# Attention and expert kernel on one core: pair 30's score inputs and pair 26's probabilities moved ahead in the hand-written lead-in table, pair 32's scaling moved behind

## Chip, cores and metric

The kernel runs on one core of a Trainium2 chip. The metric is the time of one execution on the device in microseconds (us); the kernel before has a median of 714.67 us over three runs.

## What is computed

Banded attention with a few global keys, then a feed-forward layer with a rational activation, all in float32:

```python
# q, k, v: (4, 8, 768, 64); n_global = 8, n_local = 96
rel = pos[:, None] - pos[None, :]
keep = (pos[None, :] < n_global) | ((rel >= 0) & (rel < n_local))
scores = scale * (q @ k.T) - slopes[h] * dist        # dist = |rel|, n_local for far global keys
a = softmax(where(keep, scores, -1e9)); x = a @ v
x = x.transpose(0, 2, 1, 3).reshape(3072, 512)
# the feed-forward layer: d_model 512, d_ff 2048
h = x @ w_in
P = a[0] + a[1]*h + a[2]*h*h + a[3]*h**3
Q = 1 + |b[0]|*|h| + |b[1]|*h*h
out = (P / (Q + 1e-6)) @ w_out
```

## The kernel before

The 3072 tokens are 12 chunks of 256. A chunk has eight attention units (two token tiles by four pairs of heads; units are numbered 0 to 95) and eight feed-forward steps (128 x 2 columns of `d_ff` each, numbered 0 to 95 as well). From unit 24 on two units are handled together and named by the even one: "pair 30" is units 30 and 31, four heads of one token tile. The feed-forward of a chunk runs about one chunk behind its attention, so TensorE has large matmuls to do while the softmax of later pairs is made on the other engines.

What happens to one such pair u, with the words of the table that names each stage:

- `L` loads q and k into `nat` (lines 179, 180); `V`, `vp` load v.
- `sp` (`st_split`): POOL scales q in `nat` (line 505), then DVE transposes `nat` in 32 x 32 blocks into `sp` (line 508).
- `zw` (`st_scatter`, line 516): SP sends `sp` to a DRAM buffer `zq` in four transfers. `sr` (`st_gather`, line 523): SP reads it back as `qk`, the layout that the score matmuls want. There are two `zq` buffers, used by turns.
- `s` (`st_score`, line 598): 56 small matmuls (32 for the first tile of a batch) from `qk` into PSUM. `t` (line 633): DVE adds the mask, takes the row's extreme. `x` (line 642): ACT's exponential. `r` (lines 647, 649): DVE's sum and reciprocal. `n` (line 655): POOL scales the probabilities `pr`.
- `T` (`st_pT`, line 675): DVE transposes `pr` in blocks. `tw` (`st_spread`, line 686): SP sends them to DRAM buffer `z` in four transfers. `P` (`st_pTE`, line 702): SP reads them back as `pT`.
- `o` (line 721): the matmuls of two pairs with v; `y`, `z` (lines 750, 760) make the two-part `xh`, `xl` that feeds the feed-forward steps.

One feed-forward step f: `f1` (line 340, 24 matmuls into `h`), `e1` (lines 372 to 374, ACT), `e2` (381, 382, DVE), `eq` (386, POOL, in a few steps DVE: `SUM_V`), `e3` (397, 398, ACT), `e4` (402 to 404, DVE), `gh` (412, ACT), `gl` (415, POOL or DVE), then `f2` (line 442, six matmuls for each of the two token tiles) two steps later. The result of step f that `f2` waits for is called g18, g19 and so on here, the sum of `eq` fa18, the step's PSUM result h18.

What sets the order: PE and SP execute in the order in which the program issues their work. Until step 30 of the main loop the order on ACT, DVE and POOL is written by hand too: `LEAD` is one string of words, each word a stage of a unit, read left to right under `manual_schedule`. What the table has issued, the loop skips (`part` keeps a set `done`). From then on a scheduler places the work of ACT, DVE and POOL by the priorities in `PRI`, with `behind` holding the scaling `sp` behind the last `eq` or `gl` on POOL once `paced["on"]` is set.

The end of the table is where the chunk's first pairs of the new kind (24, 26, 28, 30, 32) pass through these stages while the feed-forward steps 14 to 18 run. Lines of the change: the last three lines of `LEAD` (78 to 80), and line 859, `paced["on"]`.

Of the kernel before, what the change touches and what calls it, by code (L numbers as in the profile page):

```python
# [34 lines left out]
FIXED = 30  # L35
# [39 lines left out]
f1_1_5_1 z20 li23 e4_1_4 T23 e1_1_5 P23 s24 li13 t24 f2_0_7_0 t25 sr26 eq_1_5 e2_1_5 x24 f2_0_7_1 e3_1_5  # L75
ho11 lo9 o22 O0_0 lo11 f1_1_6_0 y22 O0_1 gh_1_4 z22 ho12 D0_1 gl_1_4 e4_1_5 f1_1_7_0 f1_1_7_1 r24 D0_0
n24 gh_1_5 f1_1_6_1 gl_1_5 e1_1_7 lo10 f2_1_4_0 e1_1_6 eq_1_7 L30 e2_1_7 e2_1_6 f2_1_4_1 L32
x25 eq_1_6 f1_2_0_0 r25 lo12 e3_1_6 f1_2_0_1 n25 e4_1_6 s26 t26 f2_1_5_0 x26 t27 T24 tw24 sr28 r26 ho13 e3_1_7 n26 lo13 f1_2_1_0 e1_2_0 e4_1_7 f2_1_5_1 eq_2_0 gh_1_6 f1_2_1_1 s28 x27 gl_1_6 e3_2_0 r27 P24
f2_1_6_0 e2_2_0 n27 kG26 t28 x28 e1_2_1 e4_2_0 f2_1_6_1 eq_2_1 e2_2_1 f2_1_7_0 f2_1_7_1 gh_2_0 gl_2_0 O1_0 O1_1
r28 n28 sp30 zw30 D1_0 T26 tw26 ho14 lo14 V28 D1_1 V30 V32 ho15 lo15  # L80
"""


# [59 lines left out]
def tile_kernel(ctx: ExitStack, tc: tile.TileContext, q, k, v, n_global, n_local,  # L143
# [202 lines left out]
    paced = {}  # L346
# [4 lines left out]
    def behind(engine):  # L351
        return tc.issue_after(paced[engine]) if paced.get("on") else nullcontext()
# [6 lines left out]
    def plain(f):  # L359
        return (f < FPC or divmod(f, FPC) in PLAIN) and not pl.split  # L360
# [62 lines left out]
    def cut_of(c):  # L423
        return HALF if c < 2 and not pl.split else FPC
# [281 lines left out]
    def run_of(u):  # L706
        return 4 if u >= PAIRS else 2
# [56 lines left out]
    def windowed():  # L764
# [26 lines left out]
        def part(kind, *args):  # L791
            if (kind, *args) not in done:
                done.add((kind, *args))
                parts[kind](*args)

        def token(word, final=False):
            kind = word[:2] if word[:2] in parts else word[0]
            rest = word[len(kind):]
            if kind == "BL":
                part(kind)  # L800
                return
            if kind in "Wabcdhl":
                part(kind, (1, int(rest[1]), int(rest[2])) if rest[0] == "i" else (0, int(rest[1:])))
                return
            args = [int(x) for x in rest.split("_") if x]
            if not final and kind in ("f1", "f2", "e1", "e2", "eq", "e3", "e4", "gh", "gl"):
                args = [FPC * args[0] + args[1], *args[2:]]
            part(kind, *args)
# [10 lines left out]
        for t in range(NU + LAG + F2):  # L819
            k = t - LAG  # L820
            u0 = t - 3 - run_of(t - 4)

            def on(name, u, *kinds):
                if 0 <= u < NU:
                    tc.cur_priority = base + 1000 * t + PRI[name]
                    for kind in kinds:
                        part(kind, u)

            def ffn(name, k, kind, *args):
                if 0 <= k < NU:  # L830
                    tc.cur_priority = base + 1000 * t + PRI[name]
                    part(kind, steps[k], *args)

            def ffn2(name, k, x):
                if 0 <= k < NU:
                    c, j = divmod(steps[k], FPC)
                    tc.cur_priority = base + 1000 * t + PRI[name]
                    part("f2", steps[k], x)
                    if j == cut_of(c) - 1 and j < FPC - 1:
                        part("H", c, x)  # L840
                    if j == FPC - 1:
                        part("O", c, x)
                        if c < NCH - 1:
                            late.append((c, x))
                        else:
                            part("D", c, x)

            def on_send(c, x):
                tc.cur_priority = base + 1000 * t + PRI["load"]
                part("D", c, x)  # L850

            if k == NU - 2:
                with tc.manual_schedule(engines={mybir.EngineType.Activation, mybir.EngineType.DVE, mybir.EngineType.Pool, mybir.EngineType.SP}):
                    for n, word in enumerate(TAIL.split()):
                        tc.cur_priority = base + 1000 * t + n
                        token(word, True)
                break
            fixed = t >= FIXED
            paced["on"] = t >= FIXED
            if t % 2:  # L860
                on("gather", t + 1, "sr")
                on("load", t + 3, "zw")
                on("load", t - 3, "P")
            else:
                on("load", t + 6, "L")
                on("load", t, "V")
                on("load", t - 2, "vp")
            if t < FIXED:
                on("score", t - 2, "s", "kg", "t")
                on("soft", t - 2, "x", "r")  # L870
            if fixed and t % 2:
                on("score", t - 1, "s", "t")
                on("score", t, "t")
                if u0 % 4 == 0:
                    on("pv", u0, "o")
                    on("x", u0, "y", "z")
            ffn("ffn1a", k, "f1", 0)
            if t < FIXED:
                on("qkT", t, "qT")
                if u0 % run_of(t - 4) == 0:  # L880
                    on("pv", u0, "o", "vg")
                    on("x", u0, "y", "z")
                on("qkE", t, "qE", "kG")
            ffn("ew3", k - 1, "e3")
            if t < FIXED:
                on("norm", t - 2, "n")
            ffn("ffn1b", k, "f1", 1)
            ffn("ew1", k, "e1")
            ffn("ew4", k - 1, "e4")
            if 0 < k <= NU and not plain(steps[k - 1]):  # L890
                ffn("ew4", k - 1, "gh")
                ffn("ew4", k - 1, "gl")
            ffn("ew2", k, "e2")
            ffn("ew2", k, "eq")
            if t % 2 == 0:
                with behind(mybir.EngineType.Pool):
                    on("split", t + 4, "sp")
                    on("split", t - 2, "kG")
            if fixed:
                on("score", t - 1, "t")  # L900
                for u in (t - 1, t) if t % 2 else (t - 1,):
                    on("soft", u, "x", "r")
                    on("norm", u, "n")
            on("pT", t - 2, "T", "tw")
            for c, x in late:
                on_send(c, x)
            late.clear()
            if t < FIXED:
                on("pT", t - 3, "P")
            ffn2("ffn2a", k - F2, 0)  # L910
            ffn2("ffn2b", k - F2, 1)
            for key in [(1, ct, jw) for jw in range(4) for ct in range(NCT)] + [(0, ft) for ft in range(NFT)] if t == FIXED else ():
                tc.cur_priority = base + 1000 * t + PRI["wsplit"]
                for kind in "Wabcdhl":
                    part(kind, key)
# [99 lines left out]
    with ExitStack() as es:  # L1015
        pl.dram = es.enter_context(tc.tile_pool(name="dram", bufs=1, space=bass.MemoryType.DRAM))
        zs[:] = [pl.dram.tile([2 * P, NB * P], F32, tag=f"z{n}", name=f"z{n}", bufs=1) for n in range(2)]
        zqs[:] = [pl.dram.tile([P, NB, P], F32, tag=f"zq{n}", name=f"zq{n}", bufs=1) for n in range(2)]
        pl.ldp = es.enter_context(tc.tile_pool(name="ldp", bufs=2))
        pl.att = es.enter_context(tc.tile_pool(name="att", bufs=2))  # L1020
        pl.ffn = es.enter_context(tc.tile_pool(name="ffn", bufs=2))
        pl.ps_h = es.enter_context(tc.tile_pool(name="ps_h", bufs=2, space=PSUM))
        pl.ps_o = es.enter_context(tc.tile_pool(name="ps_o", bufs=2, space=PSUM))
        pl.ps_r = es.enter_context(tc.tile_pool(name="ps_r", bufs=1, space=PSUM))
        pl.ps_t = es.enter_context(tc.tile_pool(name="ps_t", bufs=3, space=PSUM))
        windowed()
# [51 lines left out]
```

## Time and profile before

| what | value |
|---|---|
| median of 3 runs | 714.67 us (713.19, 714.67, 715.09) |
| the profiled execution's own time | 712.47 us |
| its span, first to last instruction | 710.7 us |
| mean granted TensorE clock | 0.985 of full speed |
| busy: PE, DVE, ACT, POOL | 671.8, 537.8, 532.3, 361.9 us |

The profile is of one execution, by a hardware profiler. Times in its views are in us from the start of the span. "Idle before" is the time in which the engine had nothing running, with the instruction that ended it; that releaser is inferred, and where several things were waited for the last one by the profile is named. SPq is the queue of transfers that SP issues: its rows are the issues, and the landing comes later.

### The profile page before, as it was taken

The page shows a single profiled execution, that of the slowest core. Times are in us where ns is not written, and L with a number is a line of the kernel's source. Part 1 is how long each engine was busy: PE and PEld are TensorE (multiplying, and loading weights), DVE is VectorE, ACT ScalarE, POOL GpSimd, SP SyncE. Part 2 cuts the span into 40 slices and gives each one's busy share as a digit, 9 for nine tenths or more (in the row PEclk, how much of TensorE's full clock was granted, in tenths as well). Part 3 has the DMA queues.
Part 4 walks back from the last instruction along what each step waited for, and adds up shares of the span by engine and source line. Part 5 has one row for each costly group of instructions (what it writes and reads, how often), then busy time and mean ns, then how long its engine had stood idle before and what let it go on. Part 6 is the DMA issues. An engine that isn't in the chain of part 4 may idle for free.

```text
span 710.7 us, 17118 instructions
## 1 busy us (share of the span) xinstructions
PE 671.8 (95%) x6167; PEld 576.8 (81%) x6167; DVE 537.8 (76%) x1319; ACT 532.3 (75%) x1174; POOL 361.9 (51%) x487
## 2 busy tenths in 40 slices
PE   5799997999939999999999999999999999999995
PEld 4577776868738898888888898888888888899995
DVE  6898996897856777777778778778687777766664
ACT  6899998686727787787777777777777777776763
POOL 2444546565434555555565455546555456444441
PEclk9999999899979999999999999999999999999998
DMA  8874554412177567475376584674566755420001
GB/s 197 260 216 109 171 157 133 128 44 62 40 198 169 141 166 174 124 201 137 88 187 142 134 219 120 148 196 107 131 162 159 175 135 149 126 88 1 30 1 36
DMA packets 161215, 95.22 MB, mean 134 GB/s; under 512 B 100064, under 2 KB 141152, under 8 KB 161120
## 3 DMA queue, kind: packets, MB, share of 16 engines
q1 hardware_dynamic: 161120, 94.02, 51.0%
q8 instruction: 51, 0.84, 0.5%
q14 instruction: 44, 0.36, 0.2%
HBM read 66.39 MB, written 27.59 MB: 132 GB/s over the span
## 4 chain that ended last, share of the span: by engine, by line
PE 79%; ACT 11%; DVE 3%; issue 2%; SPq 2%; DMA 1%; POOL 1%; POOLq 0%; ACTq 0%
PE h L340 33%; PE acc L442 30%; PE o L721 6%; PE s L598 4%; PE acc L438 2%; PE h L332 2%; ACT pr L642 2%; ACT r L271 1%; ACT fu L372 1%; DMA r<-in_moe_w_in_dram 1%; ACT qzero L561 1%; PE s L584 1%; ACT fs L397 1%; ACT fa L373 1%; ACT q L398 1%
## 5 line engine op out<-in xcount | busy, mean ns | idle before, releaser
L386 POOL TENSOR_TENSOR fa<-fa,fs 128x512 f32<-128x512 f32 (+1 forms) x86 | 109.8, 1277 | 161.2 <-ACT fs L374 156.8
L397 ACT ACTIVATE fs<-fa,coef 128x512 f32<-128x512 f32 (+1 forms) x97 | 69.9, 721 | 86.3 <-POOL fa L386 82.9
L655 POOL TENSOR_SCALAR pr<-pr,stats 128x160 f32<-128x160 f32 (+2 forms) x170 | 67.9, 417 | 127.8 <-DVE stats L649 75.9
L442 PE MATMUL acc<-wout_h,g 128*128 128x512 f32 x352 | 117.1, 393 | 0.7 <-POOL g L415 0.7
L402 DVE SCALAR_TENSOR_TENSOR fu<-fu,coef,q 128x512 f32<-128x512 f32 (+1 forms) x97 | 71.7, 739 | 60.2 <-ACT q L398 59.8
L415 POOL TENSOR_TENSOR g<-fu,g 128x512 fp32r<-128x512 f32 x84 | 107.9, 1285 | 15.4 <-ACT g L412 11.5
L442 PE MATMUL acc<-h,g 128*128 128x512 f32 x336 | 110.7, 391 | 0.0
L340 PE MATMUL h<-xh,win_h 128*128 128x256 f32 x352 | 101.8, 289 | 0.2 <-DVE fu L382 0.2
L340 PE MATMUL h<-xh,h 128*128 128x256 f32 x352 | 101.2, 287 | 0.0
L340 PE MATMUL h<-xl,win_h 128*128 128x256 f32 x352 | 98.7, 280 | 0.6 <-DVE xl L760 0.6
L340 PE MATMUL h<-xl,h 128*128 128x256 f32 x352 | 98.4, 280 | 0.0
L642 ACT ACTIVATE pr<-pr,stats 128x160 f32<-128x160 f32 (+2 forms) x192 | 82.6, 433 | 17.7 <-DVE stats L633 17.7
L372 ACT ACTIVATE fu<-h,coef 128x512 f32<-128x512 f32 x94 | 73.0, 776 | 27.7 <-PE h L340 26.5
L381 DVE TENSOR_TENSOR fu<-fu,h 128x512 f32<-128x512 f32 (+1 forms) x97 | 65.8, 678 | 35.6 <-ACT fs L374 34.5
L442 PEld LDWEIGHTS acc<-wout_h,g 128*128 128x128 f32 x352 | 66.1, 188 | 13.3 <-POOL g L415 1.2
L382 DVE SCALAR_TENSOR_TENSOR fu<-fu,coef,h 128x512 f32<-128x512 f32 (+1 forms) x97 | 71.2, 734 | 2.7
L442 PEld LDWEIGHTS acc<-h,g 128*128 128x128 f32 x336 | 63.1, 188 | 11.9 <-issue 0.2
L403 DVE SCALAR_TENSOR_TENSOR q<-fa,coef,q 128x512 f32<-128x512 f32 (+1 forms) x97 | 72.2, 744 | 0.0
L340 PEld LDWEIGHTS h<-xh,win_h 128*128 128x128 f32 x352 | 66.4, 189 | 4.6 <-issue 1.9
L340 PEld LDWEIGHTS h<-xh,h 128*128 128x128 f32 x352 | 66.2, 188 | 4.2 <-issue 2.8
L340 PEld LDWEIGHTS h<-xl,win_h 128*128 128x128 f32 x352 | 66.5, 189 | 2.1 <-DVE xl L760 0.8
L404 DVE SCALAR_TENSOR_TENSOR fu<-q,fu 128x512 f32<-128x512 f32 (+1 forms) x97 | 66.3, 683 | 2.2
(262 smaller groups left out, 1683.2 us busy)
## 6 DMA issues: line engine op xcount, KB each, us to landing
pT<-z SPq DMA_DIRECT2D x30, 512.0 KB, 4.1
z<-T SPq DMA_DIRECT2D x120, 80.0 KB, 2.3
zq<-sp SPq DMA_DIRECT2D x144, 64.0 KB, 1.8
qk<-zq SPq DMA_DIRECT2D x36, 256.0 KB, 2.8
r<-in_moe_w_in_dram SPq DMA_DIRECT2D x16, 512.0 KB, 5.3
r<-in_moe_w_out_dram SPq DMA_DIRECT2D x16, 512.0 KB, 3.9
nat<-in_q_dram SPq DMA_DIRECT2D x48, 128.0 KB, 4.3
nat<-in_k_dram SPq DMA_DIRECT2D x48, 128.0 KB, 4.2
```

The lines of the kernel that those rows point to most:

```text
L340: nc.tensor.matmul(out=h_of(f, y), lhsT=w[:, fs], rhs=x[:, ct, :], start=(n == 0), stop=(n == 3 * NCT - 1))
L372: nc.scalar.activation(out=u, in_=h, func=AF.Identity, scale=a3, bias=a2)
L382: nc.vector.scalar_tensor_tensor(out=u, in0=u, scalar=a1, in1=h, op0=ALU.add, op1=ALU.mult)
L386: pace(side(f, SUM_V).tensor_tensor(out=a, in0=a, in1=s, op=ALU.add))
L397: nc.scalar.activation(out=s, in_=a, func=AF.Ln, bias=q1)
L402: nc.vector.scalar_tensor_tensor(out=u, in0=u, scalar=a0, in1=r, op0=ALU.add, op1=ALU.mult)
L403: nc.vector.scalar_tensor_tensor(out=r, in0=a, scalar=q1, in1=r, op0=ALU.add, op1=ALU.mult)
L404: nc.vector.scalar_tensor_tensor(out=u, in0=r, scalar=2.0, in1=u, op0=ALU.subtract, op1=ALU.mult, reverse0=True)
L415: pace(side(f, G_V, f == NU - 1 and ys == 1).tensor_tensor(out=gs[f][:, 1, ys], in0=ew[f]["u"][:, ys], in1=gs[f][:, 0, ys], op=ALU.subtract))
L442: nc.tensor.matmul(out=acc, lhsT=gs[f][:, z, y, ts], rhs=w, start=(start and n == 0), stop=(stop and n == 2))
L642: nc.scalar.activation(out=d, in_=d, func=AF.Exp, scale=-1.0, bias=st[:, x:x + 1], accum_out=st[:, 2 + 2 * x:3 + 2 * x])
L655: (nc.vector if u < NORMS else nc.gpsimd).tensor_scalar(out=d, in0=d, scalar1=st[:, 6 + x:7 + x], scalar2=0.0, op0=ALU.mult, op1=ALU.add)
```

## The change

The table's words are permuted and a few are added. `sp30 zw30` (pair 30's scaling, transpose and scatter) move from the table's last line to the start of its third last, right behind the loads `L30` and `L32`. `P24` (which stood at the end of that line) and a new `sr30` (pair 30's gather) stand right behind `sr28`. `T26 tw26` move from the last line up behind `t28`, and a new `P26` with them. In the kernel before, `sr30` and `P26` were not in the table and came from the main loop. The pacing of `sp` starts two loop steps earlier; step 28's `sp32` is then held behind the last `eq` or `gl` on POOL.

```diff
-x25 eq_1_6 f1_2_0_0 r25 ... T24 tw24 sr28 r26 ho13 ... e3_2_0 r27 P24
-f2_1_6_0 e2_2_0 n27 kG26 t28 x28 e1_2_1 ... O1_0 O1_1
-r28 n28 sp30 zw30 D1_0 T26 tw26 ho14 lo14 V28 D1_1 V30 V32 ho15 lo15
+sp30 zw30 x25 eq_1_6 f1_2_0_0 r25 ... T24 tw24 sr28 P24 sr30 r26 ho13 ... e3_2_0 r27
+f2_1_6_0 e2_2_0 n27 kG26 t28 T26 tw26 P26 x28 e1_2_1 ... O1_0 O1_1
+r28 n28 D1_0 ho14 lo14 V28 D1_1 V30 V32 ho15 lo15
...
-            paced["on"] = t >= FIXED
+            paced["on"] = t >= FIXED - 2
```

PE's order does not change. On SP, at the end of the table (`zq1` holds pair 30, `zq0` pairs 28 and 32; `z0` is pair 24, `z1` pair 26), before:

```order
L523 DMA qk_64<-zq0_87 128x512
L702 DMA pT24_2167<-z0_85 128x512
L516 DMA zq1_88<-sp30_2219 32x4x128 x4
L482 DMA out_0_dram<-o1_0_2210 128x512
L686 DMA z1_86<-T26_2226 32x128
...
L180 DMA nat34_2247<-in_k_dram 128x4x64
L523 DMA qk_64<-zq1_88 128x512
L516 DMA zq0_87<-sp32_2251 32x4x128 x4
L702 DMA pT26_2258<-z1_86 128x512
```

and now:

```order
L516 DMA zq1_88<-sp30_1999 32x4x128 x4
L686 DMA z0_85<-T24_2076 32x128
...
L523 DMA qk_64<-zq0_87 128x512
L702 DMA pT24_2083<-z0_85 128x512
L523 DMA qk_64<-zq1_88 128x512
L686 DMA z1_86<-T26_2191 32x128
...
L702 DMA pT26_2197<-z1_86 128x512
L482 DMA out_0_dram<-o1_0_2226 128x512
```

Pair 30's scatter now leads this stretch of the queue, its gather stands third behind pair 24's spread, and pair 26's probabilities are read back ahead of both output stores and the loads `vt28`, `vt30`, `vt32` and `nat34`. Pair 32's scatter follows those loads.

On DVE, what now stands at pair 30's transpose (behind the polynomial of step 14, `fu14`), at pair 26's, and at the arithmetic of step 18 (`fa18` to the last use of `fu18`, in which the transpose of pair 34 and pair 30's totals lie):

```order
L382 SCALAR_TENSOR_TENSOR fu14_1974<-fu14_1974,coef_60,h14_1888 128x512
L508 STREAM_TRANSPOSE sp30_1999<-nat30_1981 128x4x4x32
L647 TENSOR_REDUCE stats_59<-stats_59 128x2
...
L675 STREAM_TRANSPOSE T26_2191<-pr26_2063 128x4x4x32
...
L386 TENSOR_TENSOR fa18_2295<-fa18_2295,fs18_2296 128x512
L290 TENSOR_TENSOR w0_15l_2247<-w0_15f_1670,h0_7_2235 128x512
...
L508 STREAM_TRANSPOSE sp34_2310<-nat34_2250 128x4x4x32
L402 SCALAR_TENSOR_TENSOR fu18_2294<-fu18_2294,coef_60,q18_2408 128x512
L403 SCALAR_TENSOR_TENSOR q18_2408<-fa18_2295,coef_60,q18_2408 128x512
L760 TENSOR_TENSOR xl3_2392<-o12_2382,xh3_2391 128x4x128
L647 TENSOR_REDUCE stats_59<-stats_59 128x2 x2
L404 SCALAR_TENSOR_TENSOR fu18_2294<-q18_2408,fu18_2294 128x512
```

Pair 30's transpose stood some 50 rows further on, pair 26's some 20. Before, the three instructions 402 to 404 of step 18 followed on the polynomial without anything between; now pair 30's four score reductions (line 633), the transpose of `nat34`, `xl3` and the totals stand ahead of the last of them. Pair 32's transpose stands now ahead of step 17's line 404; before, it stood behind it, together with those of pairs 30 and 26.

On POOL, what now stands from step 16's result g16 to step 18's g18:

```order
L415 TENSOR_TENSOR g16_2223<-fu16_2109,g16_2223 128x512
L505 TENSOR_TENSOR nat32_1995<-nat32_1995,qsc_67 128x256
L655 TENSOR_SCALAR pr28_2188<-pr28_2188,stats_59 128x160 x4
L290 TENSOR_TENSOR w0_14l_2237<-w0_14f_1482,h0_7_2235 128x512
L415 TENSOR_TENSOR g17_2303<-fu17_2201,g17_2303 128x512
L505 TENSOR_TENSOR nat34_2250<-nat34_2250,qsc_67 128x256
L655 TENSOR_SCALAR pr30_2377<-pr30_2377,stats_59 128x160 x4
L386 TENSOR_TENSOR fa19_2424<-fa19_2424,fs19_2425 128x512
L415 TENSOR_TENSOR g18_2432<-fu18_2294,g18_2432 128x512
```

Pairs 30 and 32 have changed places in the scaling (before, `nat32` stood where `nat30` now stands, behind g13), and g18 now stands behind pair 30's normalization and the sum fa19; before, it stood ahead of both, and of `nat34`. The rest of the program, from step 21 on, has the same order on every engine but for one swap of two neighbours on DVE.

## Rows read from the trace of the kernel before

**Rows 1.** Timeline of PE: start, us, then the instruction, idle before it.
```profile
194.86 0.39 PE L442 MATMUL acc<-wout_h,g 128*128 128x512 f32 x1
205.74 1.43 PE L598 MATMUL s<-qk 64*32 64x64 f32 x56 [10.49 <-DMA qk<-zq]
```
**Rows 2.** PE's waits from 230 us to the end: us, times, longest.
```profile
PE acc L451 <- DVE o L471: 0.5, 1, 0.5
```
**Rows 3.** The chain that ended last, 150 to 260 us: start, us, what.
```profile
193.74 0.72 DVE sp L508
...
202.04 3.56 DMA qk<-zq
...
205.74 1.57 PE s L598 x32
...
209.62 3.51 PE h L340 x24
```
**Rows 4.** Windows: busy us of PE, PEld, DVE, ACT, POOL, then granted clock, DMA.
```profile
205.00:210.00 5.00, 3.79 (x74) 3.25 (x75) 2.43 (x13) 2.10 (x9) 0.44 (x2) 0.50 0.84 202
```
**Rows 5.** The same chain further on, from pair 32's scores.
```profile
221.41 0.79 PE s L598 x28
...
225.19 2.73 PE acc L442 x12
...
234.26 1.96 PE o L721 x32
236.22 2.92 PE h L340 x24
```
**Rows 6.** Timeline of SP's queue of transfers: start, us of the issue.
```profile
166.22 0.51 SPq L180 DMA_DIRECT2D nat<-in_k_dram  x1
177.55 1.90 SPq L686 DMA_DIRECT2D z<-T  x4
...
180.97 0.34 SPq L702 DMA_DIRECT2D pT<-z  x1
```
**Rows 7.** Timeline of POOL.
```profile
168.70 0.61 POOL L505 TENSOR_TENSOR nat<-nat,qsc 128x256 f32<-128x256 f32 x1
...
182.63 0.72 POOL L655 TENSOR_SCALAR pr<-pr,stats 128x128 f32<-128x128 f32 x2 [0.99 <-DVE stats L649]
...
188.26 1.27 POOL L415 TENSOR_TENSOR g<-fu,g 128x512 fp32r<-128x512 f32 x1 [4.76 <-ACT g L412]
...
196.44 1.26 POOL L290 TENSOR_TENSOR w_14l<-w_14f,h 128x512 fp32r<-128x512 f32 x1
...
209.56 1.52 POOL L655 TENSOR_SCALAR pr<-pr,stats 128x160 f32<-128x160 f32 x4 [4.67 <-ACT pr L642]
```
**Rows 8.** Timeline of DVE.
```profile
173.92 0.75 DVE L402 SCALAR_TENSOR_TENSOR fu<-fu,coef,q 128x512 f32<-128x512 f32 x1 [0.86 <-ACT q L398]
...
186.88 0.69 DVE L386 TENSOR_TENSOR fa<-fa,fs 128x512 f32<-128x512 f32 x1
...
192.10 0.15 DVE L649 RECIPROCAL stats<-stats 128x2 f32<-128x2 f32 x1
...
197.19 1.06 DVE L386 TENSOR_TENSOR fa<-fa,fs 128x512 f32<-128x512 f32 x1
...
201.18 0.69 DVE L404 SCALAR_TENSOR_TENSOR fu<-q,fu 128x512 f32<-128x512 f32 x1
...
207.29 0.33 DVE L633 CUSTOM_DVE_ANT_0 pr<-s,near 128x160 f32<-128x160 f32 x1 [1.31 <-PE s L598]
```
**Rows 9.** DMA issues of the page: count, KB each, median us to landing.
```profile
pT<-z SPq DMA_DIRECT2D x30, 512.0 KB, 4.1
z<-T SPq DMA_DIRECT2D x120, 80.0 KB, 2.3
...
nat<-in_k_dram SPq DMA_DIRECT2D x48, 128.0 KB, 4.2
```
**Rows 10.** The page's busy times over the whole span.
```profile
PE 671.8 (95%) x6167; PEld 576.8 (81%) x6167; DVE 537.8 (76%) x1319; ACT 532.3 (75%) x1174; POOL 361.9 (51%) x487
```

More of the change, by code (lines that the diff above doesn't have):

```diff
@@ L77 @@
 n24 gh_1_5 f1_1_6_1 gl_1_5 e1_1_7 lo10 f2_1_4_0 e1_1_6 eq_1_7 L30 e2_1_7 e2_1_6 f2_1_4_1 L32
-x25 eq_1_6 f1_2_0_0 r25 lo12 e3_1_6 f1_2_0_1 n25 e4_1_6 s26 t26 f2_1_5_0 x26 t27 T24 tw24 sr28 r26 ho13 e3_1_7 n26 lo13 f1_2_1_0 e1_2_0 e4_1_7 f2_1_5_1 eq_2_0 gh_1_6 f1_2_1_1 s28 x27 gl_1_6 e3_2_0 r27 P24
-f2_1_6_0 e2_2_0 n27 kG26 t28 x28 e1_2_1 e4_2_0 f2_1_6_1 eq_2_1 e2_2_1 f2_1_7_0 f2_1_7_1 gh_2_0 gl_2_0 O1_0 O1_1
-r28 n28 sp30 zw30 D1_0 T26 tw26 ho14 lo14 V28 D1_1 V30 V32 ho15 lo15
+sp30 zw30 x25 eq_1_6 f1_2_0_0 r25 lo12 e3_1_6 f1_2_0_1 n25 e4_1_6 s26 t26 f2_1_5_0 x26 t27 T24 tw24 sr28 P24 sr30 r26 ho13 e3_1_7 n26 lo13 f1_2_1_0 e1_2_0 e4_1_7 f2_1_5_1 eq_2_0 gh_1_6 f1_2_1_1 s28 x27 gl_1_6 e3_2_0 r27
+f2_1_6_0 e2_2_0 n27 kG26 t28 T26 tw26 P26 x28 e1_2_1 e4_2_0 f2_1_6_1 eq_2_1 e2_2_1 f2_1_7_0 f2_1_7_1 gh_2_0 gl_2_0 O1_0 O1_1
+r28 n28 D1_0 ho14 lo14 V28 D1_1 V30 V32 ho15 lo15
 """
```

## The prediction
> **What bounds the kernel now.** I read the waits of TensorE (PE) first, because it is busy for 95% of the span [rows 10], then the chain of waits where PE stands still, then the timelines of the queues that feed it. From 230 us to the end PE waits once, for 0.5 us [rows 2]: there the time is PE's own work. Before that, one gap stands out. PE's last matmul of step 16 ends at 194.86 + 0.39 = 195.25 us, and the next thing in its order, pair 30's scores, starts at 205.74: 10.49 us of idle time, ended by the gather `qk<-zq` [rows 1]. The chain says why the gather is late: pair 30's transpose on DVE starts at 193.74 only, and behind it SP issues one transfer after another until the gather at 202.04, which lands 3.56 us later [rows 3]. SP is a single queue, so the scatter, two output stores, pair 26's spread and five loads all had to be issued first.
>
> The gap costs more than its idle time. In the window behind it the granted clock is 0.50, the lower of its two levels, after PE had stood still [rows 4]. The scores take 1.57 us and step 19's 24 matmuls 3.51 [rows 3], where pair 32's scores and a later step take 0.79 and 2.92 [rows 5].
>
> **What the gap is worth.** Take the stretch from 195.25 to pair 32's scores at 221.41: 26.16 us. In it PE does pair 30's scores, 16 matmuls of `o`, step 19, one `f2`, step 20, one `f2`. At full clock by the rows of later steps [rows 5] that is 0.79 + 0.98 (half of the 32 matmuls of 1.96) + 2.92 + 2.73 + 2.92 + 2.73 = 13.07 us. So a stretch without waits would be 26.16 - 13.07 = **13.1 us** shorter.
>
> **Part 1: pair 30's inputs ahead.** On POOL its scaling takes the place of pair 32's, which started at 168.70 and took 0.61 [rows 7]. Pair 30's k load is issued before pair 32's, whose issue at 166.22 [rows 6] had landed by 168.70, so the data is there. DVE gains one transpose of 0.72 us [rows 3] at about 172.7; right behind that place it now idles 0.86 us for ACT before 173.92 [rows 8]. The cover is larger than the instruction, so I take nothing; uncovered it would be 0.72 for the chain to step 14. SP gets the four issues of the scatter ahead of pair 24's spread. SP waits there for `T24` until 177.55 and four issues take 1.9 us [rows 6], so they fit between 173.5 and 175.4: nothing, and if the transpose came late each us beyond 2 would go into everything behind it. The gather is now issued behind pair 24's read, which goes out at 180.97 and takes 0.34 [rows 6]. It starts near 181.4 and with the 3.56 us of [rows 3] lands at 185. PE wants it at 195.25. Ten microseconds of slack: the wait disappears.
>
> **Part 2: pair 26's probabilities ahead.** They are what PE wants next, for `o`, at 195.25 + 0.79 = 196.0. POOL has finished their normalization at 182.63 + 0.72 = 183.35 [rows 7]; the transpose now runs on DVE between pair 28's reductions, near 184.2 to 184.9. Spread: four issues, 1.9 us, to 186.8; landing 2.3, to 189.1; read back, 4.1, to 193.2 [rows 6, 9]. Slack 2.8 us. While SP waits for the spread to land, the output stores stand behind it; their data is ready near 190 anyway, since DVE's last piece of it ends just before 192.10 [rows 8].
>
> **Part 3: what DVE pays.** Pair 26's and pair 32's transposes now run ahead of DVE's reciprocal at 192.10 [rows 8], each some 0.65 (0.72 less the overlap with the next): the reciprocal moves to about 193.4. DVE has no idle time there to swallow it. The same transposes, and pair 30's, are gone behind it.
>
> **Part 4: what is late next.** With the gap gone, step 18's result g18 is wanted early: 195.25 + 0.79 + 0.98 + 2.92 + 2.73 + 2.92 = 205.6. Before, PE asked for it only 2.73 us ahead of pair 32's scores, at 218.7 [rows 5], long after DVE had done its part at 201.87 [rows 8]. Now I follow it:
> - DVE from 193.6 (reciprocal done): a cast, pair 28's transpose (which waits some 0.5 us for POOL's normalization of that pair) and one arithmetic pass, about 2 us in all. Before, these and three transposes filled 193.74 to 197.19 [rows 3, 8]: 3.45 less 3 x 0.65 = 1.5, plus the 0.5. Then fa18 starts at 195.6.
> - From fa18's start to the end of step 18's line 404 was 197.19 to 201.87, 4.7 us [rows 8]. Into this now fall pair 30's four reductions (0.33 each, pipelined to about 1.0 [rows 8]), pair 34's transpose 0.65, `xl` 0.65 and the totals 0.2: 2.5. That gives 195.6 + 4.7 + 2.5 = 202.8, and 203.0 with the reciprocals.
> - POOL's order puts pair 30's four normalizations, 1.52, the sum fa19, about 1.27 like its other large operations, and then g18 itself, 1.27 [rows 7]: 203.0 + 4.06 = **207.1**.
>
> So PE waits 207.1 - 205.6 = 1.5 us for g18. I estimate 0 to 3 for this term: below nothing it cannot go, and each input above may be half a microsecond out. The next one, g19, is wanted 9 us later, and its chain is shorter than that, so I expect no second wait. From step 21 on the order is the old one.
>
> One rule bears on this term. In the trace fa18 took 1.06 us while POOL ran `w_14l` at 196.44, and the like sum took 0.69 at 186.88, when POOL was idle up to 188.26 [rows 7, 8]: overlap costs 0.37, and my 4.7 us contains it once. The Trainium skill, SBUF — State Buffer, section "Who interferes with whom", says that a VectorE instruction with two SBUF inputs contends with a GpSimd one that reads SBUF, and that the shared port is held for a whole instruction, the loser blocking. By that rule both two-input passes of step 18 (fa18 and `w_15l`) could lose a full POOL operation each, and the sum would end at 704.9, as the third case below does; the row shows 0.37, not a full block.
>
> **The sum.** 13.1 - 1.5 = 11.6 us off the profiled execution: 712.47 - 11.6 = 700.9. The median of the runs, 714.67, stands 2.20 above that execution, so I forecast **703.1 us**.
>
> **The rivals.**
> 1. *No new wait.* If ACT and DVE run through step 18 a little faster than I have it, the full 13.1 comes: 714.67 - 13.1 = 701.6. For it: fa19's place ahead of g18 costs nothing if pair 30's totals come 1.5 us sooner. Against: DVE has hardly a hole there.
> 2. *The port costs more.* If each of the two passes of step 18 is held for a whole POOL operation (1.27 instead of 0.37), g18 is 1.8 later: 703.1 + 1.8 = 704.9. For it: POOL is busier beside DVE than before. Against: the 1.06 row.
> 3. *Pair 34's load is late.* Its transpose now stands inside step 18's arithmetic. The load is issued at about 195.4, behind two stores and three loads. Pair 32's landed within 2.5 us [rows 6, 7], the median over the kernel is 4.2 [rows 9]. At 4.2 and 0.6 for the scaling DVE would get it at 200.2, about 1 us late; with the DMA queues full (share 0.84 in [rows 4]) perhaps 3 late: 706.
> 4. *The gap stays or only moves.* If pair 26's read were late by as much as the gather was, PE would stop at `o` instead. To bring the gain under 0.3% it would have to wait there for 13.1 - 2.1 = 11 us, 14 with the slack of 2.8; nothing that I find in the queue ahead of it is that long. It would end within 0.3% of before, near 714.
> 5. *Slower: the wait for g recurs.* Perhaps the gap is what lets DVE and POOL catch up, and without it each pair of steps waits as g18 does. There are 39 pairs of steps from 18 to 95. 13.1 / 39 = 0.34 us for each pair cancels the gain, and at 1.5 it would be 714.67 - 13.1 + 58 = 760. For it: g18 is indeed late. Against: the chain of a step starts when its own matmuls end, so a head start is not carried along; the later order is unchanged, ran 480 us with a single wait of 0.5 [rows 2], and DVE is busy for 76% only [rows 10], so it regains a microsecond within a few.
>
> **How the numbers follow.** The forecast, a wait of 0.7 to 2.5 us, gets 0.55; no wait 0.15; the port 0.12; the late load or something like it, ending between 706 and 712, 0.11; the gap that stays 0.03; slower 0.04. About 0.3%, 2.1 us, can be told from no change, so all but the last two are faster: 0.93, 0.03 and 0.04. The range takes in the first three cases and most of the fourth; the lowest run stood 1.5 below the median, so it reaches from 701.6 - 1.3 = 700.3 up to 707.0.
>
> **What would show it.** In the profile of the changed kernel PE's wait for `qk<-zq` before pair 30's scores is gone; the granted clock stays at its upper level from 195 to 215; SP's gather for pair 30 goes out near 181; pair 32's scores start near 209.8 where they started at 221.41; and PE waits once, 1 to 2 us, for POOL's `g` near 205. Wrong would be: a wait of several microseconds at `o` (part 2), DVE standing at `sp` for a load at 172 or at 199 (part 1, rival 3), or waits for `g` that go on behind 215 (rival 5).

## The result and the profile after

The changed kernel has a median of **702.97 us** (702.53 to 703.84 over four runs), the kernel before, on the same chip, 714.53. The ratio is 0.984, 95% interval 0.983 to 0.986: 11.6 us less, where 703.1 us was forecast.

The timeline of PE (start, us, instruction, idle before it) answers to [rows 1]:

```profile
196.59 0.92 PE L598 MATMUL s<-qk 64*32 64x64 f32 x56
197.44 1.09 PE L721 MATMUL o<-pT,vt 128*64 128x128 f32 x16
198.46 0.38 PE L340 MATMUL h<-xh,win_h 128*128 128x256 f32 x1
...
201.29 0.39 PE L442 MATMUL acc<-wout_h,g 128*128 128x512 f32 x1
...
206.85 0.39 PE L442 MATMUL acc<-wout_h,g 128*128 128x512 f32 x1
207.08 0.39 PE L442 MATMUL acc<-w_4l,g 128*128 128x512 f32 x1
208.64 0.72 PE L442 MATMUL acc<-wout_h,g 128*128 128x512 f32 x2 [1.18 <-POOL g L415]
...
211.15 0.92 PE L598 MATMUL s<-qk 64*32 64x64 f32 x56
```

Pair 30's scores and the 16 matmuls of `o` follow on step 16 with no idle time, where PE stood for 10.49 us. One new wait of 1.18 us stands in their place, for POOL's `g`. This execution came to the spot 1.4 us later than the profiled one of before (its last `f2` matmul of step 16 ends at 196.66, that of before at 195.25), so times behind are compared from there. The list of PE's waits from 140 to 240 us (us in total, times, longest) has no other new one:

```profile
PE s L598 <- DMA qk<-zq: 1.2, 1, 1.2
PE acc L442 <- POOL g L415: 1.2, 1, 1.2
PE h L340 <- DVE fu L382: 0.2, 1, 0.2
```

The first is pair 28's scores at 183.6, ahead of the place of the gap; the kernel before has that wait too (1.35 us at 182.26). The windows answer to [rows 4] (busy us of PE, PEld, DVE, ACT and POOL, granted clock, DMA share):

```profile
195.00:200.00 5.00, 5.00 (x93) 4.16 (x92) 4.33 (x6) 2.54 (x5) 4.06 (x5) 1.00 0.72 170
200.00:205.00 5.00, 5.00 (x34) 4.52 (x34) 5.00 (x19) 4.88 (x14) 0.43 (x2) 1.00 0.72 158
205.00:210.00 5.00, 3.82 (x26) 3.19 (x25) 1.73 (x4) 2.60 (x5) 3.58 (x5) 1.00 0.77 202
```

PE is busy throughout but for the wait, DVE has become the full engine between 200 and 205 us, and the clock stays at its upper level, 1.00 instead of 0.50. The work that the gap slowed runs at full speed now. From pair 30's scores to `o` it is 0.85 us by the starts above, where [rows 3] have 1.57 for these scores; step 19's 24 matmuls take 2.83 us (198.46 to 201.29) instead of 3.51. The 16 matmuls of `o` take 1.09 us; before, on PE's timeline, they took

```profile
207.65 1.97 PE L721 MATMUL o<-pT,vt 128*64 128x128 f32 x16 [0.48 <-PE s L598]
```

Behind the new wait the chain has the rest of step 18's `f2`, pair 32's scores and step 21's matmuls:

```profile
208.64 2.58 PE acc L442 x10
211.22 0.79 PE s L598 x29
212.01 2.99 PE h L340 x24
```

From the end of step 16 to pair 32's scores it is now 211.22 - 196.66 = 14.56 us; it was 26.16. Between pair 32's and pair 34's scores 0.4 us is given back. There POOL's `g` of step 20 comes late by a little: in the chain it ends at 221.08, and PE's matmul follows at 221.13.

```profile
219.82 1.26 POOL g L415
221.09 0.04 issue
221.13 2.56 PE acc L442 x10
```

From pair 34's scores to the end of the span it is 701.3 - 223.62 = 477.7 us; it was 710.7 - 233.40 = 477.3. What was gained was gained in the one stretch.

### The profile page after: what moved, and what is told of

Same layout as the page of the kernel before. It is cut to its first block, busy times and chain, and to the rows that moved or that the text cites. A ratio compares the mean times of both kernels' runs of the same rounds, so it can differ in the third digit from the quotient of the medians.

```text
span 701.3 us, 17124 instructions
## 1 busy us (share of the span) xinstructions
PE 670.5 (96%) x6167; PEld 574.7 (82%) x6167; DVE 536.6 (77%) x1319; ACT 531.4 (76%) x1174; POOL 361.4 (52%) x487
## 4 chain that ended last, share of the span: by engine, by line
PE 74%; ACT 10%; DVE 8%; POOL 2%; issue 2%; DMA 1%; SPq 1%; DVEq 0%; POOLq 0%
PE h L340 30%; PE acc L442 30%; PE o L721 5%; PE s L598 3%; PE h L332 2%; ACT pr L642 2%; PE s L584 1%; DVE q L403 1%; DVE fu L402 1%; DMA r<-in_moe_w_in_dram 1%; DVE fu L404 1%; DVE pr L633 1%; ACT r L271 1%; ACT qzero L561 1%; ACT fs L397 1%
```

## The experiments

There were eleven runs, each beside the kernel before on the same chip: nine new kernels, one of them twice, and the change once more. Beside the medians one measure is used, from PE's own timeline, in which it matters less how an execution fell: **the stretch** from the moment when PE wants pair 30's scores (their start less the idle time before them) to the start of pair 34's scores. It is 233.40 - 195.25 = 38.2 us before and 223.62 - 196.59 = 27.0 us after. The change gives 26.8 in its second trace (the last table), so a few tenths between two traces say little.

### Each half of the change alone

Pair 30 alone (pair 26's words put back on the table's last line):

```diff
-... kG26 t28 T26 tw26 P26 x28 ...
-r28 n28 D1_0 ho14 ...
+... kG26 t28 x28 ...
+r28 n28 D1_0 T26 tw26 ho14 ...
```

> The change with part 2 undone: pair 26's transpose and spread back on the table's last line, its read left to the main loop. Theory (both parts are needed, because PE's order wants pair 30's scores and pair 26's probabilities within a microsecond of each other): no wait before pair 30's scores, but TensorE (PE) stops at the matmuls of o instead, since pair 26's read now stands behind two stores, five loads and pair 32's scatter on SP and goes out near 202, landing near 206: a wait of 8 to 10 us, and a lower granted clock behind it; 710 to 714 us. Rival (pair 30's gather alone made the gap; pair 26's read was late in the kernel before only because it had time): o waits under 2 us, 703 to 705 us.

708.92 us (706.73 to 710.48), ratio 0.993, 0.991 to 0.995. PE's timeline:

```profile
194.41 0.92 PE L598 MATMUL s<-qk 64*32 64x64 f32 x56
202.82 1.98 PE L721 MATMUL o<-pT,vt 128*64 128x128 f32 x16 [7.49 <-issue]
```

and the windows:

```profile
195.00:200.00 5.00, 0.33 (x23) 0.16 (x12) 5.00 (x16) 3.08 (x10) 0.62 (x1) 0.94 0.87 220
200.00:205.00 5.00, 2.18 (x17) 1.88 (x18) 2.14 (x5) 0.79 (x2) 3.38 (x6) 0.50 0.86 214
```

The scores start without a wait, and the gap moves to `o`. The view names no releaser ("issue"), but SP's queue does: pair 26's read goes out at 199.88, behind pair 32's scatter, and PE goes on 2.9 us later. The wait was a little shorter than the 8 to 10 us expected, and the time 1 us below the 710 to 714 expected.

Pair 26 alone (pair 30's words put back):

```diff
-sp30 zw30 x25 ...  sr28 P24 sr30 r26
-r28 n28 D1_0 ho14 ...
+x25 ...  sr28 P24 r26
+r28 n28 sp30 zw30 D1_0 ho14 ...
```

> The change with part 1 undone: pair 30's scaling, transpose and scatter back on the table's last line and its gather left to the main loop; pair 26's stages stay ahead. Theory: the gap stays where it was, 9 to 11 us before pair 30's scores, ended by the gather, with the lower granted clock behind it, and o no longer waits the 0.3 to 0.5 us behind the scores: 712 to 715 us. Rival (what filled SP's queue was pair 26's spread and read, and with those gone the gather comes early by itself): gap under 5 us, 708 us or less.

711.7 us (708.03 to 713.15), ratio 0.995, 0.994 to 0.997. PE's timeline:

```profile
206.12 1.43 PE L598 MATMUL s<-qk 64*32 64x64 f32 x56 [9.53 <-DMA qk<-zq]
```

and SP's ahead of it, pair 30's scatter and gather:

```profile
196.53 1.75 SPq L516 DMA_DIRECT2D zq<-sp  x4
...
202.10 0.53 SPq L523 DMA_DIRECT2D qk<-zq  x1
```

The gap is where it was, and the median just under the 712 to 715 us expected. The halves are worth 5.2 and 2.4 us by themselves, 11.6 together: PE wants both inputs within 0.8 us of each other, so either one that is late keeps much of the gap.

### Does the gather's place count, or the scatter's?

Only the word `sr30` taken out of the table; the gather then comes from the loop, behind the loads of pair 34.

```diff
-... sr28 P24 sr30 r26 ...
+... sr28 P24 r26 ...
```

> The change without the one word sr30: pair 30's scatter goes out early, but its gather stands where the main loop puts it, behind two stores and five loads. Theory (a late place in SP's single queue is enough to make the gap): the gather goes out near 197 to 198 instead of 182.8 and lands 3 to 4 us later, so PE waits 4 to 6 us before pair 30's scores; 707 to 710 us. Rival (the late transpose was the cause, the queue only followed): wait under 1.5 us, 702 to 704 us.

702.18 us (700.53 to 704.39), ratio 0.982, 0.980 to 0.984: not told apart from the change. PE's timeline:

```profile
199.59 0.92 PE L598 MATMUL s<-qk 64*32 64x64 f32 x56 [2.46 <-DMA qk<-zq]
```

and the window behind it:

```profile
200.00:205.00 5.00, 5.00 (x85) 4.64 (x67) 4.27 (x14) 2.10 (x7) 0.94 (x1) 1.00 0.64 148
```

My expectation of 707 to 710 us missed: the wait lies between the two that I had named, the time where the rival had it. The gather was issued at 196.29 instead of 182.76, 13.5 us later, and PE stood for 2.46 us; the clock did not fall. The wait for `g18` is gone in this version: the scheduler put step 18's work ahead of pair 30's on DVE and POOL, so one wait took the place of the other. The stretch is 28.0 us, 1.0 more than the change's. This kernel and the one with pair 26 alone differ only in the place of `sp30 zw30`, and on one chip they take 702.18 and 711.7 us: the early scatter (with the scaling and transpose ahead of it) carries the gain. PE wanted the scores 0.5 us later in this execution (197.13 and 196.59), so of the gather's 13.5 us some 10.5 are slack.

### Is pair 32's holding back needed?

```diff
-            paced["on"] = t >= FIXED - 2
+            paced["on"] = t >= FIXED
```

> The change without the earlier pacing: pair 32's scaling and transpose run as soon as the scheduler places them (POOL right behind pair 30's, DVE 20 instructions earlier). Theory (holding pair 32 back is worth nothing by itself; its transpose only costs DVE 0.65 us wherever DVE is full): within 0.3% of the change; PE's wait for g18 shrinks from 1.2 to 0.6 us, as DVE has one transpose less between 192 and 203. Rival (held back so that DVE's chain to steps 14 to 17 is not delayed): a new PE wait of 0.5 us or more between 175 and 195, 704 us or more.

701.24 us (699.96 to 702.12), ratio 0.981, 0.979 to 0.984; stretch 26.3, the wait for `g18` 0.85, where 0.6 was expected. The change itself has 0.86 in its second trace, so the wait did not shrink by this. The one difference that fits the edit is small: PE's wait for `h` at 172 us is 0.46 us instead of 0.19. By itself this line of the change brings nothing that shows in the time (but see the third row of the last table).

### The wait for g18: which engine is behind it?

Three kernels move one operation each between POOL and DVE. First `g18` itself, to DVE:

```diff
-G_V = ((0, 1), (0, 2), (1, 2), (0, 5), (1, 6), (1, 7))
+G_V = ((0, 1), (0, 2), (1, 2), (0, 5), (1, 6), (1, 7), (2, 2))
```

> The change with step 18's subtraction g18 on DVE instead of POOL, where it stands behind pair 30's four normalizations and fa19. Theory (the new wait of 1.2 us is POOL's queue): g18 is done near 206.5 on DVE (its 1.36 us of the like row, behind line 404 and one pass of step 19), before PE wants it at 207.3; that wait is gone, and as DVE's work for step 19 shifts by 1.3 us, g19 may come up to 0.5 us late: 701.7 to 702.9 us, 0 to 1.2 us below the change. Rival (DVE, not POOL, is the bound behind 200 us): the wait only moves to g19 or g20, 1 us or more, same time as the change or later.

704.6 us (702.64 to 704.83), ratio 0.986, 0.984 to 0.988; stretch 27.7. Timeline of PE:

```profile
209.77 0.92 PE L598 MATMUL s<-qk 64*32 64x64 f32 x56
...
214.93 0.50 PE L442 MATMUL acc<-wout_h,g 128*128 128x512 f32 x1 [1.31 <-ACT g L412]
216.28 0.73 PE L442 MATMUL acc<-wout_h,g 128*128 128x512 f32 x2 [0.62 <-POOL g L415]
```

There is no wait ahead of 209.77, but 1.31 + 0.62 us stand one step later, at step 19's `f2`. The time expected was missed, and the wait is the rival's, though not for the rival's reason: DVE is not full there. Its timeline has 2.99 us of idle time ahead of the first of these rows:

```profile
210.36 0.69 DVE L381 TENSOR_TENSOR fu<-fu,h 128x512 f32<-128x512 f32 x1 [2.99 <-ACT fs L374]
...
213.57 0.65 DVE L404 SCALAR_TENSOR_TENSOR fu<-q,fu 128x512 f32<-128x512 f32 x1
```

The scheduler, which places the work here, has put both passes of step 20's polynomial (lines 381, 382) and pair 36's transpose ahead of step 19's line 404, which ends at 214.22; in the change's trace only the first of these three stands ahead of it, and it ends at 212.49. ACT waits 1.81 us for that line before it can make its part of `g19`.

Then step 17's `g`, some 10 us earlier on POOL (197.02 and 207.31 in the change's trace), to DVE:

```diff
-G_V = ((0, 1), (0, 2), (1, 2), (0, 5), (1, 6), (1, 7))
+G_V = ((0, 1), (0, 2), (1, 2), (0, 5), (1, 6), (1, 7), (2, 1))
```

> The change with step 17's subtraction g17 on DVE behind fa18, so that POOL runs nothing while DVE runs fa18 (its next work waits for a load until about 199). A test of why fa18 took 1.67 us in the changed kernel, 1.06 before and 0.69 elsewhere. Theory (it is held until the POOL instruction that runs beside it has ended, then takes its 0.69): fa18 takes 0.65 to 0.75 us where POOL is idle beside it, and if POOL's w_14l still runs, fa18 ends about 0.6 us behind it. Rival (the length comes from elsewhere, as ACT's writing of its input): 1.4 us or more though POOL is idle. Time: g17's 1.3 us on DVE costs as much as it saves; 702 to 705 us.

700.47 us (two runs, 700.05 and 700.89), ratio 0.981, 0.979 to 0.983; stretch 25.7, and the list of PE's waits from 190 to 230 us is empty. DVE's timeline:

```profile
195.98 0.68 DVE L386 TENSOR_TENSOR fa<-fa,fs 128x512 f32<-128x512 f32 x1
196.58 0.68 DVE L415 TENSOR_TENSOR g<-fu,g 128x512 fp32r<-128x512 f32 x1
197.18 0.69 DVE L290 TENSOR_TENSOR w_15l<-w_15f,h 128x512 fp32r<-128x512 f32 x1
```

and POOL's beside it:

```profile
194.57 1.29 POOL L290 TENSOR_TENSOR w_14l<-w_14f,h 128x512 fp32r<-128x512 f32 x1
197.93 0.61 POOL L505 TENSOR_TENSOR nat<-nat,qsc 128x256 f32<-128x256 f32 x1 [2.07 <-DMA nat<-in_q_dram]
202.57 1.29 POOL L386 TENSOR_TENSOR fa<-fa,fs 128x512 f32<-128x512 f32 x1 [4.02 <-ACT fs L374]
203.84 1.52 POOL L655 TENSOR_SCALAR pr<-pr,stats 128x160 f32<-128x160 f32 x4
205.32 1.30 POOL L415 TENSOR_TENSOR g<-fu,g 128x512 fp32r<-128x512 f32 x1
```

DVE has one operation more and is done sooner, so the 702 to 705 us expected missed, while the theory of the hold came true: `fa18` takes 0.68 us here, with POOL idle beside it, and 1.67 us in the changed kernel, where POOL runs `g17`. DVE's timeline of the changed kernel:

```profile
197.16 1.67 DVE L386 TENSOR_TENSOR fa<-fa,fs 128x512 f32<-128x512 f32 x1
198.75 0.68 DVE L290 TENSOR_TENSOR w_15l<-w_15f,h 128x512 fp32r<-128x512 f32 x1
```

and POOL's:

```profile
197.02 1.26 POOL L415 TENSOR_TENSOR g<-fu,g 128x512 fp32r<-128x512 f32 x1
199.13 0.78 POOL L505 TENSOR_TENSOR nat<-nat,qsc 128x256 f32<-128x256 f32 x1 [0.85 <-DMA nat<-in_q_dram]
```

`fa18` ends at 198.83, 0.55 us after `g17`'s end at 198.28. From `fa18`'s start to the end of step 18's line 404 DVE takes 6.75 us with `g17` and 7.15 without it. `g18` ends 0.8 us sooner, 10.64 us behind `fa18`'s start instead of 11.43. DVE gives half of that. The other half goes with POOL's order: the scheduler now puts `fa19` ahead of pair 30's normalization, in time in which POOL had nothing to do; in the change it stands behind.

Third, `fa18` to POOL:

```diff
-SUM_V = (..., (1, 2), (2, 2), (1, 3), ...)
+SUM_V = (..., (1, 2), (1, 3), ...)
```

> The change with step 18's sum fa18 on POOL instead of DVE, between w_14l and g17. Theory (DVE's filled stretch from 192 to 204 makes g18 late, 1.67 us of it by fa18 held beside POOL): fa18 runs on POOL in 1.3 us, DVE reaches the end of step 18's line 404 about 1 us earlier, near 203, pair 30's normalizations and g18 follow 1 us earlier, and PE's wait for g18 falls from 1.2 to 0 to 0.4 us: 701.8 to 702.8 us. Rival (the wait is POOL's length alone): POOL has 1.3 us more to do ahead of g17 and the wait for g18 stays 1 us or more; 703 us or more.

701.27 us (700.07 to 702.76), ratio 0.982, 0.981 to 0.984; stretch 26.5, wait 0.71. Neither the 0 to 0.4 us of the theory nor the rival's 1 us came, and 0.71 is close to the change's second 0.86. What the run does show is that the hold goes with the overlap, not with the line. Now `w_15l` meets POOL's `fa18`, on DVE's timeline

```profile
196.38 1.68 DVE L290 TENSOR_TENSOR w_15l<-w_15f,h 128x512 fp32r<-128x512 f32 x1
```

and on POOL's:

```profile
196.24 1.27 POOL L386 TENSOR_TENSOR fa<-fa,fs 128x512 f32<-128x512 f32 x1
197.48 1.74 POOL L415 TENSOR_TENSOR g<-fu,g 128x512 fp32r<-128x512 f32 x1
```

Again DVE ends 0.55 us after POOL (198.06 and 197.51), and POOL's next operation, which starts while DVE is at it, takes 1.74 us instead of 1.27.

### The best version, and two controls

The change itself, the version with `g17` on DVE once more, that version with pair 32 not held back, and `g17` on DVE in the kernel before ran on one chip, five rounds.

> The change as it is, beside the versions below on one chip. Theory: the retained wait for POOL's g18 of about 1.2 us stays, and the median stands near 703 us, 11.6 below before; 702.5 to 703.9.

> Step 17's last operation on DVE, again. Theory: POOL's queue reaches g18 in time, so the wait of 1.18 us ahead of step 18's f2 is gone, and the stretch from the wanted start of pair 30's scores to pair 34's scores is 25.7 us against 27.0 in the change: the median is 1.3 us lower, near 701.5, in fast intervals 0.5 to 2.5 lower. Rival: that difference is only how two executions fell, and both medians agree within 0.5 us.

> Both at once: step 17's last operation on DVE, and pair 32's scaling not held back. Each alone left little or no wait for g18. Theory: a wait that is gone cannot be gained twice, so the stretch to pair 34's scores is 25.5 to 26.0 us and the median that of the version with step 17's operation on DVE alone, within 0.5 us. Rival: pair 32's transpose now stands ahead on DVE, which the other operation has loaded already, so that a wait for g18 of 0.5 to 1 us comes back and the median is that much higher.

> The kernel before, with step 17's last operation on DVE and nothing else. Theory: in the kernel before no result g is waited for at this place, since PE stands for 10.5 us at pair 30's gather and DVE and POOL are done with step 18 long before; so the edit gives nothing, within 0.5 us of before, or delays that gather a little (DVE has 0.7 us more to do around pair 30's transpose): 0 to 0.7 us slower. Rival: the edit is worth 1.4 us by itself, whatever the order of the table.

| kernel | median, us (lowest to highest) | ratio to before, interval | stretch, us |
|---|---|---|---|
| the change | 701.35 (701.22 to 702.88) | 0.983, 0.981 to 0.985 | 26.8 |
| with `g17` on DVE | 699.61 (698.75 to 700.51) | 0.980, 0.978 to 0.982 | 25.7 |
| and pair 32 not held back | 701.16 (699.98 to 702.5) | 0.982, 0.980 to 0.984 | 26.2 |
| before, with `g17` on DVE | 713.59 (710.99 to 715.55) | 0.999, 0.998 to 1.001 | 39.1 |

The change's median is 1.6 us lower here than in the first comparison, below the 702.5 to 703.9 expected, and 12.7 us below the kernel before; its wait for `g18` is 0.86 instead of 1.18. The kernel before moved by 0.4 only, so the gain is 11.6 in one comparison and 12.7 in the other; the intervals of the two ratios overlap.

With `g17` on DVE the slowest of five runs (700.51) lies below the fastest of the change (701.22). The medians are 1.7 us apart, of which the stretch holds 1.1; the other 0.7 stands in the two traces already at 155 us, far ahead of the moved operation (`w_8l` on POOL starts at 155.79 and 155.09), so the traces don't show it as the edit's work. That version has the lowest median of all. In the kernel before the same edit gives nothing: there is no wait for `g` to remove, and the gap of 10 us is still there.

Not holding pair 32 back, on top, costs 1.5 us by the medians (one run of five overlaps), more than my expectation of either kind. In its trace a wait of 0.37 us for `g18` is back, POOL has pair 30's normalization ahead of `fa19` again, and a wait for `h` at 172 us is 0.46 instead of 0.19; these make 0.8 us (0.5 of it in the stretch), of which pair 28's scores give back 0.25 by a shorter wait. So some 0.6 us of the 1.5 can be put down to the edit; 1.1 us stands in the two traces already at 155 us, ahead of all that the edit moves, and why the medians differ by more than 0.6 stays open.

## Why the prediction was right

Times of the forecast are moved by the 1.4 us by which this execution came later.

- **What the gap is worth** held: PE's work behind it runs at full clock, and 26.16 - 14.56 = 11.6 us, wait included, is the forecast sum to a tenth.
- **Part 1** held. Pair 30's transpose lies in DVE's idle time, of which 0.28 us is left (0.86 in [rows 8]); the scatter is on SP at 174.93, ahead of `T24`; the gather goes out at 182.76 (forecast 181.4 + 1.4 = 182.8). Its slack of ten microseconds was measured too: issued 13.5 us later, with PE 0.5 us later, it came 2.46 late, which makes 10.5.
- **Part 2** held: pair 26's spread ends at 188.2 (186.8 + 1.4), its read goes out at 189.57, 0.9 us sooner than reckoned (189.1 + 1.4). That `o` would be next to stop without it is shown by the first experiment.
- **Part 3** held: the reciprocal is at 194.68; 192.10 + 1.3 + 1.4 = 194.8.
- **Part 4** held in the total, by two errors that cancel in its middle. `fa18` starts at 197.16 (197.0), line 404 ends at 204.31 (204.2), and `g18` ends on POOL at 208.59 (207.1 + 1.4 = 208.5):

```profile
204.57 1.53 POOL L655 TENSOR_SCALAR pr<-pr,stats 128x160 f32<-128x160 f32 x4 [4.67 <-DVE stats L649]
206.06 1.30 POOL L386 TENSOR_TENSOR fa<-fa,fs 128x512 f32<-128x512 f32 x1
207.31 1.28 POOL L415 TENSOR_TENSOR g<-fu,g 128x512 fp32r<-128x512 f32 x1
```

  **The reading that failed** is that overlap with POOL costs `fa18` "0.37, not a full block". In [rows 7, 8] `w_14l` ends at 197.70 and `fa18` at 198.25: 0.55 us apart, as in every pair above. The kernel before had shown it twice more, on `w_4l` at 111 us (1.13 us instead of 0.68) and on step 14's `g` at 181 us (1.36), which also end 0.55 and 0.54 us behind POOL's operation; I had read one pair alone. DVE waits until POOL's operation has ended and then does nearly all of its own; the 1.06 are the 0.51 us that were left of `w_14l` when `fa18` came, and 0.55; 0.37 was no price of overlap, but how these two happened to meet.

  So the rule of the Trainium skill, SBUF — State Buffer, section "Who interferes with whom", which I set against the row, is borne out: the lock lasts for the whole instruction, and lines 403 and 404, which read one operand from PSUM, take their usual 0.75 and 0.69 us beside POOL in this trace (at 180.62 and 181.41), as that section's rule for a single SBUF input has it.

  The second rival was therefore right in kind, for one pass: `fa18` took 0.61 us more than the 1.06 that my 4.7 held, where that rival had 0.9. It was not paid twice, since `w_15l` began ahead of POOL's next operation, the scaling of `nat34`, which took 0.78 us instead of 0.61; and the 0.22 us that DVE had idled ahead of line 402, 0.13 us between lines 403 and 404 that other work now fills, and 0.16 us less for the inserted work (2.34 for my 2.5) took back most of it.
- **The wait** costs 1.64 us where 1.5 was reckoned, of which 1.18 is PE's idle time. Step 18's `f2` starts at 206.85 (205.6 + 1.4 = 207.0), and only its third matmul needs POOL's part of `g`, so two run ahead of the wait; the twelve end at 211.22, 4.37 us later, where 2.73 is the time without a wait.
- **No second wait** held for `g19`; for `g20` some 0.3 us came that I did not have. Then it ends, and so the slower rival fell: 477.7 us remain behind pair 34's scores, against 477.3.
- **Pair 34's load** was in time: POOL has scaled it at 199.91, and DVE takes it at 200.99 without a wait. It was not a quick load: the one of q is issued at 195.01, 1.8 us sooner than reckoned (195.4 + 1.4), and POOL can start at 199.13, 4.1 us later. The 2.5 us of the third rival set the issue of pair 32's k against the scaling of its q; from the issue of q (165.67) it is at most 3.0.
- **The median** came out right partly by luck. For the profiled execution I had 700.9 us, and it took 703.09: 2.2 us more, as much as the 2.20 that I then added for the distance from execution to median. The change's profiled execution stands at its median, 702.97. The stretch lost 11.1 us, but the two executions differ by 9.4 (712.47 and 703.09), mostly because this one came to the gap 1.3 us later. In the executions traced PE wants pair 30's scores between 194.4 and 197.1 us, in the order of before (195.25 and 196.98) and with the change (196.59 and 195.35) alike, so that spread is no sign of the change.
- **The range** has a slip: the lowest run stood 1.5 us below the median, and I took 1.3 off. With 1.5 its lower end would be 700.1.

## What to carry to other kernels

A gap that one late input ends may have a second input waiting behind it: here the halves of the move gave 5.2 and 2.4 us by themselves, both together 11.6. What a gap is worth is the stretch up to the next undisturbed landmark less the work in it at full clock, and the work that the gap hid has then to be followed engine by engine to the new wait. Where DVE is the engine behind that wait, look at what POOL runs beside its two-input operations: one operation given to DVE made DVE earlier, by 0.4 us.

## What the runs showed that I had not expected

- **The lock between DVE and POOL, to a few hundredths of a microsecond.** A 128x512 DVE operation with both operands in SBUF that starts while POOL runs ends 0.54 to 0.56 us after POOL's operation ends, whatever its start: it takes 1.06, 1.10, 1.36, 1.67 or 1.68 us in all, and 0.68 alone. Only where POOL has no more than 0.1 us left is nothing lost: in the trace of before, at 101.14 and 132.16 us, DVE takes 0.68 and 0.69 and ends 0.58 and 0.59 behind POOL. POOL is held in turn: `g17` 1.74 for 1.27 us, the scaling of `nat34` 1.06 for 0.61 with the late gather.
- **The clock and the length of a stop.** PE's stop of 2.46 us left the granted clock at 1.00; behind stops of 7.49 and 9.53 us the windows show 0.50, the lower level.
